# An activation tile laid out by 128-token chunks, with three additions moved from VectorE to accumulating transfers

## The chip, the cores and the metric

The kernel runs on one core of one Trainium2 chip. The metric is the device time of one execution in microseconds (us), as the median of several executions.

In the profile, PE is TensorE's matmuls, PEld its weight loads, DVE is VectorE, ACT is ScalarE, POOL is GpSimd, SP is SyncE. "L1024" is line 1024 of the kernel at hand; inserted lines shift the numbers by a few lines between kernels.

## The reference, cut to what matters

```python
# x: (1, 2048, 512), F = 1792; all in bfloat16
xn  = layernorm(x)
Bu  = einsum("bld,pd->blp", xn, B_bar)                # complex, P = 512
h_t = Lam_bar * h_{t-1} + Bu_t                        # complex scan over 2048 tokens
y   = 2 * einsum("blp,dp->bld", h, C).real + xn * Dskip
out = x + y + (silu(xn @ w1) * (xn @ w3)) @ w2
```

The kernel treats the tokens as 4 blocks of 512. Per block, the two last products, C against the states and w2 against the gates, are one long product against an "act" tile that holds 22 pieces of 128 features: the gates `silu(..)*(..)` and the real and imaginary states. Its tokens are taken as "pairs" of two 128-token chunks, 8 pairs (n = 0 to 7), two per block.

## The kernel before

A pair's product is a 2 x 2 block product done with seven products of half size in place of eight, as in Strassen's method. The left factors need sums of quarters of the act tile: S3 = A11 - A21, S2 = S3 - A22, S1 = A21 + A22 (in place) and S4 = A12 + S2 (in place on A12, so only after product 2 has read A12). Product 3 reads S4.

```python
act_blk[b] = actp.tile([P, 2 * NK, TBLK], FP16, name="act")      # 128 x 22 x 512
...
def post_c(...):                           # second part of the states, after the scans
    ...                                    # (last half of block 3: on VectorE)
        gp.dma_start(out=a, in_=p16, accum_op=ALU.add)          # "states transfer"
...
def res_list(b):                           # residual: xn*Dskip + x
    def mul(): ...                         # VectorE
    def add():
        gp.dma_start(out=xn_blk[b], in_=x_blk[b], accum_op=ALU.add)   # "residual transfer"
...
def difference(b):                         # VectorE, on the result of the residual transfer:
                                           # even chunks less odd ones, on half of the columns
    ...
        nc.vector.tensor_tensor(out=o[:, 0::2, D2]..., in0=o[:, 0::2, D2], in1=o[:, 1::2, D2], op=ALU.subtract)
...
def row_sums(n, b, p):                     # S3, S1, S2 of a pair; S3 and S2 are
    ...                                    # written over x_blk or tw
def product2():
    mms(f, v["a12"], weight(1, D1), False)
    v["s4"] = v["a12"]
    if n == 5:
        gp.dma_start(out=v["s4"], in_=v["s2"], accum_op=ALU.add)
    else:
        nc.vector.tensor_tensor(out=v["s4"], in0=v["a12"], in1=v["s2"], op=ALU.add)
```

VectorE's work of the second half of block 0 and of what follows is queued in this order (cut):

```python
ssm_tasks(0)                    # ... ends with block 0's second states transfer
...
res_tasks(0)                    # multiply, then the residual transfer of block 0
for which in (2, 0, 1): weight_sum(0, which)
res_tasks(1)
...
bg.add(*difference(0))          # needs the residual transfer of block 0
first_sums = row_sums(0, *pairs[0])
...
for i, which in ((0, 3), (1, 2), (1, 0), (1, 1), (1, 3)): weight_sum(i, which)
```

## Time and profile before

| | before |
|---|---|
| median (lowest to highest) | 201.86 us (201.84 to 201.89), 3 runs |
| profiled span | 200.1 us |
| busy: PE, DVE, ACT, POOL | 98, 91, 67, 25% of the span |
| packets of GpSimd's DMA queue | 9520 |

### The profile page before, as it was taken

To read this page: it belongs to the slowest core of one execution; us is meant where nothing else is said; L and a number is where in the kernel's file an instruction comes from. 1 tells how busy PE (TensorE), PEld (TensorE's weight loads), DVE (VectorE), ACT (ScalarE), POOL (GpSimd) and SP (SyncE) were. 2 spreads that over 40 slices of the span, in tenths; PEclk is the share of its full clock that TensorE was granted. 3 is DMA by queue.
4 is the path that set the end of the run, shared out by engine and by line. 5 is a ranking of instruction groups with operands and counts; after the bars stand their busy time and mean duration, and the time that the engine had idled before them with its cause. 6 is when DMAs were issued, how large, how long until landed. Compare 5 with 4: busy or idle time off the path is not lost.

```text
span 200.1 us, 3642 instructions
## 1 busy us (share of the span) xinstructions
PE 196.5 (98%) x1377; PEld 128.6 (64%) x1377; DVE 181.9 (91%) x255; ACT 133.9 (67%) x277; POOL 49.8 (25%) x71
## 2 busy tenths in 40 slices
PE   8999999999999999999999999999999999999994
PEld 2874444444444488854444468888566668888893
DVE  3699699999999999989999999899999999899862
ACT  3799797699999987967796684362588783111220
POOL 7170279700310132243015013100033103130000
PEclk9999999999999999999999999999999999999999
DMA  6999997990474033944876955560159901994111
GB/s 150 328 276 224 292 168 139 338 268 2 92 147 79 0 65 69 160 131 92 147 140 122 98 101 46 58 135 3 52 105 143 141 2 13 101 142 74 56 41 43
DMA packets 35651, 23.94 MB, mean 120 GB/s; under 512 B 23217, under 2 KB 33585, under 8 KB 35633
## 3 DMA queue, kind: packets, MB, share of 16 engines
q0 software_dynamic: 9520, 10.20, 34.8%
q1 hardware_dynamic: 25536, 13.21, 27.0%
q10 hardware_dynamic: 576, 0.30, 0.7%
q8 instruction: 11, 0.18, 0.4%
q14 instruction: 8, 0.06, 0.1%
HBM read 7.74 MB, written 2.10 MB: 49 GB/s over the span
## 4 chain that ended last, share of the span: by engine, by line
PE 96%; DMA 1%; DVE 1%; SPq 0%; issue 0%; DVEq 0%
PE gu_ps L555 34%; PE gu_ps L982 17%; PE y_ps L982 10%; PE gu_ps L775 7%; PE bu_ps L982 7%; PE y_ps L440 5%; PE bu_ps L440 5%; PE y_ps L797 3%; PE gu_ps L587 2%; PE gu_ps L700 2%; DMA x_blk<-in_A_x_dram 1%; PE bu_ps L797 1%; PE y_ps L700 1%; PE bu_ps L587 1%; PE y_ps L243 1%; PE bu_ps L700 0%
## 5 line engine op out<-in xcount | busy, mean ns | idle before, releaser
L555 PE MATMUL gu_ps<-xnT,w_sb 128*128 128x512 bf16 x312 | 68.2, 379 | 0.0
L555 PEld LDWEIGHTS <-w_sb 128*128 128x128 bf16 x312 | 30.4, 98 | 36.5
L982 PEld LDWEIGHTS <-act 128*128 128x128 f16 x462 | 43.5, 98 | 5.4
L565 ACT ACTIVATE u<-gu_ps 128x512 bf16<-128x512 f32 x41 | 24.8, 605 | 5.8 <-PE gu_ps L555 5.4
L564 ACT ACTIVATE g<-gu_ps 128x512 bf16<-128x512 f32 x41 | 24.7, 603 | 5.1 <-PE gu_ps L555 5.0
L488 DVE TENSOR_TENSOR_SCAN u<-rho,ends,u 128x512 bf16<-128x512 f32 x16 | 19.9, 1270 | 0.0
L507 POOL DMA_DIRECT2D act<-p x7 | 6.4, 908 | 47.1 <-DVE act L498 36.8
L440 PEld LDWEIGHTS <-bt 128*128 128x128 bf16 x96 | 9.4, 98 | 11.3
L982 PE MATMUL gu_ps<-w_sb,act 128*128 128x256 bf16 (+3 forms) x126 | 15.9, 267 | 0.0
L775 PE MATMUL gu_ps<-xnT,w_sb 128*128 128x512 bf16 x64 | 15.9, 379 | 0.0
L573 DVE TENSOR_TENSOR act<-g,u 128x1024 f16<-128x1024 bf16 x21 | 14.2, 678 | 0.0
L787 ACT ACTIVATE g<-gu_ps 128x512 bf16<-128x512 f32 x14 | 8.4, 599 | 5.4 <-PE gu_ps L775 5.0
L936 POOL DMA_DIRECT2D act<-act x4 | 7.7, 1929 | 14.6 <-DVE tw L929 13.7
L440 PE MATMUL bu_ps<-xnT,bt 128*128 128x512 bf16 x48 | 11.3, 379 | 0.0
L440 PE MATMUL y_ps<-xnT,bt 128*128 128x512 bf16 x48 | 11.3, 379 | 0.0
L1005 ACT ACTIVATE x_blk<-gu_ps 128x256 f32<-128x256 f32 (+1 forms) x9 | 3.3, 367 | 10.6 <-PE gu_ps L982 10.6
L982 PE MATMUL bu_ps<-w_sb,act 128*128 128x256 bf16 (+3 forms) x84 | 10.4, 264 | 0.0
L982 PE MATMUL gu_ps<-ct,act 128*128 128x256 f16 (+1 forms) x72 | 10.4, 267 | 0.0
L488 DVE TENSOR_TENSOR_SCAN u<-rho,act,u 128x512 bf16<-128x512 f32 x8 | 10.0, 1271 | 0.0
L494 DVE TENSOR_TENSOR p<-u,tabe 128x2048 f16<-128x2048 bf16 (+1 forms) x9 | 9.9, 1099 | 0.1
L471 DVE TENSOR_TENSOR u<-u,tabe 128x2048 bf16<-128x2048 bf16 x8 | 9.8, 1222 | 0.2
L498 DVE TENSOR_TENSOR act<-u,tabe 128x2048 f16<-128x2048 bf16 (+1 forms) x9 | 9.9, 1097 | 0.0
(189 smaller groups left out, 372.8 us busy)
## 6 DMA issues: line engine op xcount, KB each, us to landing
act<-p POOLq DMA_DIRECT2D x7, 512.0 KB, 4.7
xn<-x_blk POOLq DMA_DIRECT2D x4, 512.0 KB, 5.2
out_dram<-xn SPq DMA_DIRECT2D x15, 128.0 KB, 1.7
w_sb<-in_B_w_dram SPq DMA_DIRECT2D x1, 1792.0 KB, 8.4
w_sb<-in_B_w_dram SPq DMA_DIRECT2D x2, 768.0 KB, 6.3
act<-act POOLq DMA_DIRECT2D x4, 352.0 KB, 7.0
w_sb<-in_B_w_dram SPq DMA_DIRECT2D x4, 256.0 KB, 4.5
w_sb<-in_B_w_dram SPq DMA_DIRECT2D x2, 512.0 KB, 5.9
```

The lines of the kernel that those rows point to most:

```text
L440: nc.tensor.matmul(out=ps, lhsT=bt[:, ri, dt, pt * P:(pt + 1) * P], rhs=xnT_blk[b][:, dt, :], start=(dt == 0), stop=(dt == NDT - 1))
L471: nc.vector.tensor_tensor(out=st["g"], in0=st["g"], in1=tabe[:, psl, 0:1, :].to_broadcast(FULL), op=ALU.mult)
L488: nc.vector.tensor_tensor_scan(out=v, data0=rho[:, pt:pt + 1].to_broadcast([P, TBLK]), data1=v, initial=init, op0=ALU.mult, op1=ALU.add)
L494: nc.vector.tensor_tensor(out=st["p16"][:, :, ::-1, tsl], in0=st["g"][:, :, :, tsl], in1=tabe[:, psl, 1:3, tsl], op=ALU.mult)
L498: nc.vector.tensor_tensor(out=act_state(b, hf)[:, :, :, tsl], in0=st["g"][:, :, :, tsl], in1=tabe[:, psl, 0:1, tsl].to_broadcast([P, 2, 2, ...
L555: nc.tensor.matmul(out=ps[:, tsl], lhsT=w[:, dt, f * P:(f + 1) * P], rhs=xnT[:, dt, tsl], start=(dt == 0), stop=(dt == NDT - 1))
L564: nc.scalar.activation(out=g16[:, f % 2, :], in_=g_ps, func=ACT.Silu)
L565: nc.scalar.activation(out=u16[:, f % 2, :], in_=u_ps, func=ACT.Copy)
L573: nc.vector.tensor_tensor(out=act(b)[:, k0:k1 + 1:k1 - k0, :], in0=g16, in1=u16, op=ALU.mult)
L775: nc.tensor.matmul(out=ps, lhsT=w[:, dt, f * P:(f + 1) * P], rhs=xnT[:, dt, :], start=(dt == 0), stop=(dt == NDT - 1))
L787: nc.scalar.activation(out=g16[:, f % 2, :], in_=side(w1_sb, f), func=ACT.Silu)
L982: nc.tensor.matmul(out=out, lhsT=left[:, k, :], rhs=right[k][:, cols], start=(start and k == 0), stop=(k == NK - 1), skip_group_check=True)
```

## The change

The act tile is laid out as 4 chunks of 22 pieces of 128 tokens, so that a quarter (A11, A12, ...) becomes one run of 2816 bytes per partition instead of 11 runs of 256. This is meant to make the in-place sums cheap as accumulating transfers, so that S4 of pairs 2, 3 and 4 can leave VectorE. In pairs 2 and 3 product 2 comes ahead of product 4 to give the transfer more time. The price is that a states transfer has rows of 1024 bytes instead of 4096.

```diff
-            act_blk[b] = actp.tile([P, 2 * NK, TBLK], FP16, name="act")
+            act_blk[b] = actp.tile([P, CPB, 2 * NK, P], FP16, name="act")
...
     def act_state(b, hf):
         k = k_state(2 * hf)
-        return act(b)[:, k:k + 4, :].rearrange("p (j r) t -> p j r t", r=2)
+        return act(b)[:, :, k:k + 4, :]
...
-                a, p16 = act_state(b, hf)[:, :, :, tsl], st["p16"][:, :, :, tsl]
+                a, p16 = act_state(b, hf)[:, csl], st["p16"][:, csl]
...
-        a11, a12 = a[:, 0:NK, r1], a[:, NK:2 * NK, r1]
-        a21, a22 = a[:, 0:NK, r2], a[:, NK:2 * NK, r2]
+        a11, a12 = a[:, 2 * p, 0:NK, :], a[:, 2 * p, NK:2 * NK, :]
+        a21, a22 = a[:, 2 * p + 1, 0:NK, :], a[:, 2 * p + 1, NK:2 * NK, :]
...
-            if n == 5:
+            if n in (2, 3, 4, 5):
                 gp.dma_start(out=v["s4"], in_=v["s2"], accum_op=ALU.add)
...
-        for i in ((1, 5, 2, 6, 4, 3, 7) if b == 0 else (1, 4, 2, 6, 5, 7, 3)):
+        for i in ((1, 5, 2, 6, 4, 3, 7) if b == 0 else (1, 2, 4, 6, 5, 7, 3) if b == 1 else (1, 4, 2, 6, 5, 7, 3)):
```

The cuts are the same re-layout for the gates, the other post products of the states and the copy of the scans' last values.

More of the change, by code (lines that the diff above doesn't have):

```diff
@@ L420, in act, with act_gates, split, by_state @@
         if act_blk[b] is None:
-            act_blk[b] = actp.tile([P, 2 * NK, TBLK], FP16, name="act")
+            act_blk[b] = actp.tile([P, CPB, 2 * NK, P], FP16, name="act")
         return act_blk[b]
+    def act_gates(b, f):
+        k0, k1 = k_gate(f), k_gate(f + 1)
+        return act(b)[:, :, k0:k1 + 1:k1 - k0, :].rearrange("p c k t -> p k c t")
+    def split(v):
+        return v.rearrange("p k (c t) -> p k c t", t=P)
     def act_state(b, hf):
         k = k_state(2 * hf)
-        return act(b)[:, k:k + 4, :].rearrange("p (j r) t -> p j r t", r=2)
+        return act(b)[:, :, k:k + 4, :]
+    def by_state(v):
+        return v.rearrange("p c (j r) t -> p j r c t", r=2)
     u_blk = {}
@@ L449, in ssm_tasks, with by_chunk @@
         FULL = [P, 2, 2, TBLK]
+        def by_chunk(v):
+            return v.rearrange("p j r (c t) -> p j r c t", t=P)
         def half(hf):
@@ L485, in scan @@
                 elif b > 2:
-                    init = act_blk[b - 1][:, k_state(pt, ri), TBLK - 1:TBLK]
+                    init = act_blk[b - 1][:, CPB - 1, k_state(pt, ri), P - 1:P]
                 v = st["g"][:, j, ri, :]
@@ L489, in scan, with post_a, post_b, post_c @@
                                              initial=init, op0=ALU.mult, op1=ALU.add)
-            def post_a(tsl=slice(0, TBLK)):
+            def post_a(csl=slice(0, CPB)):
                 if "p16" not in st:
-                    st["p16"] = ssmw.tile(FULL, BF16, name="p").bitcast(FP16)
-                nc.vector.tensor_tensor(out=st["p16"][:, :, ::-1, tsl], in0=st["g"][:, :, :, tsl],
-                                        in1=tabe[:, psl, 1:3, tsl], op=ALU.mult)
-            def post_b(tsl=slice(0, TBLK)):
-                nc.vector.tensor_tensor(out=act_state(b, hf)[:, :, :, tsl], in0=st["g"][:, :, :, tsl],
-                                        in1=tabe[:, psl, 0:1, tsl].to_broadcast([P, 2, 2, tsl.stop - tsl.start]),
-                                        op=ALU.mult)
-            def post_c(tsl=slice(0, TBLK)):
-                a, p16 = act_state(b, hf)[:, :, :, tsl], st["p16"][:, :, :, tsl]
+                    st["p16"] = ssmw.tile(FULL, BF16, name="p").bitcast(FP16).rearrange(
+                        "p j r (c t) -> p (j r c t)", t=P).rearrange("p (c k t) -> p c k t", c=CPB, t=P)
+                tsl = slice(csl.start * P, csl.stop * P)
+                nc.vector.tensor_tensor(out=by_state(st["p16"][:, csl]), in0=by_chunk(st["g"][:, :, ::-1, tsl]),
+                                        in1=by_chunk(tabe[:, psl, 2:0:-1, tsl]), op=ALU.mult)
+            def post_b(csl=slice(0, CPB)):
+                tsl = slice(csl.start * P, csl.stop * P)
+                n = csl.stop - csl.start
+                nc.vector.tensor_tensor(out=by_state(act_state(b, hf)[:, csl]), in0=by_chunk(st["g"][:, :, :, tsl]),
+                                        in1=by_chunk(tabe[:, psl, 0:1, tsl]).to_broadcast([P, 2, 2, n, P]), op=ALU.mult)
+            def post_c(csl=slice(0, CPB)):
+                a, p16 = act_state(b, hf)[:, csl], st["p16"][:, csl]
                 if (b, hf) == (NBLK - 1, 1):
@@ L541, in ssm_tasks @@
         add(*post0, *scans1)
-        early, late = ([(0.6, lambda fn=fn, h=h: fn(slice(h * TH, (h + 1) * TH)), ("ssm", b)) for fn in post1]
+        early, late = ([(0.6, lambda fn=fn, h=h: fn(slice(h * CPB // 2, (h + 1) * CPB // 2)), ("ssm", b)) for fn in post1]
                        for h in range(2))
@@ L571, in gate @@
             bg.own(0.6, -0.5)
-            k0, k1 = k_gate(f - 1), k_gate(f)
-            nc.vector.tensor_tensor(out=act(b)[:, k0:k1 + 1:k1 - k0, :], in0=g16, in1=u16, op=ALU.mult)
+            nc.vector.tensor_tensor(out=act_gates(b, f - 1), in0=split(g16), in1=split(u16), op=ALU.mult)
         f0 = 0
@@ L790, in gate @@
             bg.own(0.6, -0.5)
-            k0, k1 = k_gate(f), k_gate(f + 1)
-            nc.vector.tensor_tensor(out=act(b)[:, k0:k1 + 1:k1 - k0, :], in0=tiles[0], in1=tiles[1], op=ALU.mult)
+            nc.vector.tensor_tensor(out=act_gates(b, f), in0=split(tiles[0]), in1=split(tiles[1]), op=ALU.mult)
         def product(out, left, right, start):
@@ L921, in row_sums @@
         a = act(b)
-        r1, r2 = slice(2 * p * P, (2 * p + 1) * P), slice((2 * p + 1) * P, (2 * p + 2) * P)
-        a11, a12 = a[:, 0:NK, r1], a[:, NK:2 * NK, r1]
-        a21, a22 = a[:, 0:NK, r2], a[:, NK:2 * NK, r2]
+        a11, a12 = a[:, 2 * p, 0:NK, :], a[:, 2 * p, NK:2 * NK, :]
+        a21, a22 = a[:, 2 * p + 1, 0:NK, :], a[:, 2 * p + 1, NK:2 * NK, :]
         s3, s2 = (v.bitcast(FP16).rearrange("p (k t) -> p k t", t=P) for v in homes[n % 2])
@@ L1141, in keep_ends @@
         kept.add(b)
-        nc.vector.tensor_copy(out=ends, in_=act(b).rearrange("p (h k) t -> p h k t", h=2)[:, :, NFH:NK, TBLK - 1])
+        nc.vector.tensor_copy(out=ends, in_=act(b)[:, CPB - 1].rearrange("p (h k) t -> p h k t", h=2)[:, :, NFH:NK, P - 1])
     ssm_tasks(1, between=[(0.2, lambda: keep_ends(0))])
```

## The prediction

> **What bounds the kernel now.** I read the page first, then the waits of TensorE, then the chain of waits in order of time, then the groups by shape, and last the timelines of every engine around the three pairs that change. Times on the chip: 201.86 us median, 201.84 to 201.89; the profiled span is 200.1 us, so 1.76 us lie outside it. From the page:
>
> ```profile
> PE 196.5 (98%) x1377; PEld 128.6 (64%) x1377; DVE 181.9 (91%) x255; ACT 133.9 (67%) x277; POOL 49.8 (25%) x71
> PEclk9999999999999999999999999999999999999999
> PE 96%; DMA 1%; DVE 1%; SPq 0%; issue 0%; DVEq 0%
> ```
>
> TensorE (PE) is busy 98% of the span at full clock and makes up 96% of the chain that ended last. VectorE (DVE) at 91% looks like a second bound, so the next question is whether TensorE ever waits for it. The waits of TensorE alone are one line, in the warm-up:
>
> ```profile
> PE bu_ps L196 <- PEq L1194: 0.8, 1, 0.8
> ```
>
> A busy TensorE is not yet one at its peak, so I checked the rate. Pieces of the chain, as start, length, line and count (L982 is the y products, L700 the fast Bu products of block 3 woven between them):
>
> ```profile
> 12.84 8.63 PE gu_ps L555 x40
> ...
> 117.72 1.20 PE gu_ps L982 x11
> 118.92 0.87 PE y_ps L700 x8
> 119.80 1.20 PE gu_ps L982 x11
> 121.00 0.44 PE bu_ps L700 x4
> 121.44 0.44 PE y_ps L700 x4
> 121.87 1.20 PE gu_ps L982 x11
> ...
> 126.78 2.40 PE gu_ps L982 x22
> 129.19 1.20 PE y_ps L982 x11
> ...
> 196.78 0.63 PE gu_ps L982 x11
> 197.41 0.02 issue
> 197.43 0.29 DVE xn L993
> ```
>
> 8.63/40 is 215.8 ns for a 512-column matmul, 1.20/11 is 109.1 ns for one of 256 columns. The groups by shape count 472 matmuls of 512 columns, 734 of 256 and 44 of 128 between 12.84 and 197.41 us. At (columns + 6)/2.4 ns each that is 101.87 + 80.13 + 2.46 = 184.46 us, and the chain has 197.41 - 12.84 = 184.57 us there. **All waiting of TensorE after 12.84 us adds up to 0.11 us.** Before it lies the load and the first LayerNorm, after it 2.7 us of last addition and store; the change touches neither.
>
> **What the Trainium skill says, and whether the trace agrees.** (1) "TensorE: Matmul & The Clock Gate", section Back-to-back issue gap, gives 518, 262 and 134 cycles for 512, 256 and 128 columns; the 215.8 and 109.1 ns above agree. The same section's sustained 131 ns for 512 columns is not what this trace shows, so I use the cycles. (2) "VectorE: DVE Perf Modes", section The perf-mode tier table, has a bf16 tensor_tensor of 2048 elements at 1224 ns in the 2x mode; here 1215 to 1222 ns. (3) "DMA: Bandwidth & Descriptors", section SWDGE vs HWDGE vs iDMA, says that accumulation needs a GpSimd issue; the trace has all of them on POOL. (4) The same page, section Why small descriptors are slow (HBM only), says that SBUF to SBUF transfers don't suffer from small pieces. This trace disagrees. The rates of 164 to 176 us, in 40 slices of 0.3 us:
>
> ```profile
> GB/s 27 0 0 0 0 0 0 0 0 0 0 0 0 0 0 0 0 3 81 98 99 108 108 108 105 108 106 110 187 219 167 52 9 10 17 0 218 218 218 218
> ```
>
> The long plateau near 108 is the accumulation S1 of pair 5 in 256-byte rows, the 218 at the end is the states' accumulation in 4096-byte rows.
>
> **The change, part by part.** The rows concerned, by shape:
>
> ```profile
> L1024 DVE TENSOR_TENSOR act<-act,x_blk 128x1408 f16<-128x1408 f16 x4 | 3.5, 883 | 0.0
> L1024 DVE TENSOR_TENSOR act<-act,tw 128x1408 f16<-128x1408 f16 x3 | 2.6, 883 | 1.1 <-PE bu_ps L982 0.7 <-PE gu_ps L982 0.5
> L936 POOL DMA_DIRECT2D act<-act x4 | 7.7, 1929 | 14.6 <-DVE tw L929 13.7 <-DVE u L807 0.5 <-DVE x_blk L929 0.4
> L507 POOL DMA_DIRECT2D act<-p x7 | 6.4, 908 | 47.1 <-DVE act L498 36.8 <-PE gu_ps L982 5.5 <-PE y_ps L982 4.6
> ```
>
> *Removed:* the VectorE additions S4 of pairs 2, 3 and 4, 3 x 0.883 = 2.65 us of VectorE, which falls from 181.9 to about 179.3 us. None of it is on the chain, so it is worth 0 by itself.
>
> *Layout, VectorE:* counts and element sizes stay. The innermost run becomes 128 elements of step 1. The row differences (1408 elements in runs of 128) already have such runs and take 883 to 888 ns; by the line through 678 ns at 1024 and 1216 ns at 2048 a 1408-element operation would be estimated at 680 ns + 384 x 0.525 = 880 ns. So runs of 128 cost nothing, and gates, post products and differences should keep 0.68, 1.22 and 0.88 us. Change 0.
>
> *Layout, transfers:* a row of S1 or S4 grows from 256 to 2816 bytes; a row of the states' accumulation shrinks from 4096 to 1024. With 16 engines, 108 GB/s is 37.9 ns per 256-byte row and 218 GB/s 301 ns per 4096-byte row, so as an estimate a row costs 20.4 ns + 0.0685 ns per byte. A 352 KB transfer then has 8 rows per engine of 213 ns, 1.7 us, instead of 88 of 37.9, 3.3 us. POOL's part falls from 1.93 to about 0.91 us (908 ns is the row with one piece per partition). Issue to landing: 7.0 - 1.6 - 1.0 = 4.4 us by subtraction, or 4.7 - 2.4 + 1.7 = 4.0 from the states' transfers; I take 4.0. The states' 512 KB become 32 rows per engine of 90.5 ns, 2.9 instead of 2.4 us, and POOL's part rises by 3 x 0.10 = 0.3 us: 5.5 instead of 4.7 us to landing.
>
> *Added, S4 by transfer.* Start: product 2 must have read A12. Deadline: product 3. Pair 2: product 1 (117.72, 1.20) and the woven work (0.87) put product 2 at 119.80 to 121.00. S1 of pair 3 is ahead on POOL, at 120.74, free by 121.65. S4 lands at 121.65 + 4.0 = 125.7 alone, 127.4 if it has to wait out all 1.7 us of S1's data. Product 3 starts at 127.98: 0.6 to 2.3 us to spare. Pair 3: product 2 at 131.26 to 132.46, landing 136.5, product 3 at 139.45: 2.9 us to spare. Pair 4 (its order stays, product 3 is put off into pair 5): S1 of pair 5 at 166.86, S4 at 167.8, landing 171.8 to 173.5, product 3 at 176.75: 3.2 us to spare.
>
> *Moved, product 2 ahead of 4.* Product 2 adds onto the copy that ScalarE makes of product 1. The timeline of ScalarE has these copies end at 119.39 (pair 2) and 130.85 (pair 3); product 2 would start at 119.80 and 131.26. The work woven between hides them with 0.4 us to spare each.
>
> *Deadlines that tighten:* states of block 3, first half: issued 173.37, now landing 178.1, then 178.9; TensorE reads them at 179.91. States of block 2, second half: issued 145.27, then landing 150.8; the difference that reads them starts at 151.16. Block 1: landing 105.7, read at 106.77. S1 of pair 5, needed at 175.54 and now landing at 166.86 + 7.9 = 174.8, gets room instead.
>
> Sum: at most 0.11 us to win, no stall expected: **201.86 + 0.0 = 201.9 us**.
>
> **Rivals.** *S4 lands late.* If the transfers keep 6.8 us and S1 keeps POOL for 1.93 us, S4 of pair 2 lands at 122.67 + 6.8 = 129.5, and product 3 waits 1.5 us: 203.4. For it: the spare time of pair 2 is the smallest of the three, and the one such transfer of the kernel before took 6.8 us. Against: its rows were 256 bytes, and the states' transfers with long rows took 4.7 for more bytes. *VectorE leaves its fast mode* with four-level patterns: then 14 full and 4 half post products gain about 1.07 and 0.53 us each, the 28 gates 0.53 us, together near 32 us, VectorE becomes the bound and the time nears 214. For it: no operation of the trace has that many levels, so nothing shows it; against: the differences' runs. *False waits:* states and gates now share one address range per chunk; if the program's dependency tracking took ranges as whole, a gate would wait for a 5 us transfer, which I put at 1 to 4 us in all. For it nothing but the possibility; gates at 52.22 and 54.95 ran beside a transfer begun at 51.47. *VectorE was a hidden bound* and its 2.65 us come off: 199.2, which is still within 2%; against it stands the 0.11 us.
>
> **Range and chances.** The base has a scatter of 0.05 us, and the bound allows 0.11 below it, so the low end is 201.7. Above, a missed deadline of pair 2, or of the states, would cost tenths: high end 202.5. Faster by 4 us would need matmuls removed: 0.01. Slower by 4 us needs one of the middle two rivals at its worst: 0.04. The rest, 0.95, is within 2%.
>
> **What would show it.** Right: TensorE still has no wait after the warm-up; VectorE near 179.3 us with three fewer S4 additions; S1 and S4 land in about 4 us and their POOL part is near 0.9; states' accumulation lands near 5.5 us; the 0.88, 1.22 and 0.68 us of VectorE stay. Wrong: a TensorE wait before product 3 of pair 2 (S4 late) or before product 2 of pairs 2 and 3 (copy late), post products above 1.3 us, or VectorE waiting for a transfer.

## More of the kernel before

The page's list of DMA issues names, for each kind of transfer, out<-in, the queue, the count, the size and the median time from issue to landing:

```profile
act<-p POOLq DMA_DIRECT2D x7, 512.0 KB, 4.7
xn<-x_blk POOLq DMA_DIRECT2D x4, 512.0 KB, 5.2
```

The first is the states transfer, the second the residual transfer.

## The result

| | before | after |
|---|---|---|
| median (lowest to highest) | 201.88 us (201.84 to 202.13), 4 runs | 202.85 us (202.50 to 203.16), 4 runs |
| ratio, 95% interval | | 1.0045 (1.0026 to 1.0064) |
| profiled span | 200.1 us | 201.1 us |
| VectorE busy | 181.9 us | 179.9 us |
| packets of GpSimd's DMA queue | 9520 | 6240 |

A ratio here is the mean time of one kernel's runs over that of the other's runs of the same rounds, so it is not quite the ratio of the medians quoted.

The change costs about 1 us, where 0.0 was predicted. It is within the 2% that counts as the same, and yet outside the predicted range of 201.7 to 202.5 us, and the interval of the ratio lies above 1. So there is something real to find.

**Is there a new wait?** The page of the changed kernel, its busy times and its chain of waits by engine:

```profile
PE 196.0 (98%) x1365; PEld 128.6 (64%) x1377; DVE 179.9 (89%) x252; ACT 134.2 (67%) x277; POOL 49.3 (25%) x74
...
PE 59%; DVE 17%; issue 8%; POOL 7%; DMA 6%; ACT 1%; POOLq 0%
```

TensorE is still busy 98% of the span, but the chain that ended last is no longer TensorE's alone: 17% of it runs through VectorE, 7% through GpSimd and 6% through transfers. Something between them holds TensorE up. (The page counts 12 matmuls fewer than before and as many weight loads, 1377: those are records missing from the trace, and no work was removed.) The waits of TensorE in the changed kernel (engine, instruction, what released it; total, times, longest):

```profile
PE bu_ps L196 <- PEq L1207: 0.8, 1, 0.8
PE bu_ps L995 <- DVE act L1037: 0.5, 1, 0.5
PE gu_ps L571 <- DMA xnT<-xn: 0.4, 1, 0.4
```

The first is the warm-up, which the kernel before has too. The other two are new. Their place in TensorE's timeline of the changed kernel (start, length, engine, line, operation, tiles; in brackets the idle time before it and its releaser):

```profile
74.18 1.36 PE L995 MATMUL y_ps<-tw,act 128*128 128x256 f16 x11
76.06 0.94 PE L995 MATMUL bu_ps<-w_sb,act 128*128 128x256 bf16 x7 [0.51 <-DVE act L1037]
...
87.40 5.79 PE L571 MATMUL gu_ps<-xnT,w_sb 128*128 128x512 bf16 x25 [0.36 <-DMA xnT<-xn]
```

The same two places in the kernel before:

```profile
74.46 1.36 PE L982 MATMUL y_ps<-tw,act 128*128 128x256 f16 x11
75.66 0.93 PE L982 MATMUL bu_ps<-w_sb,act 128*128 128x256 bf16 x7
...
86.47 6.86 PE L555 MATMUL gu_ps<-xnT,w_sb 128*128 128x512 bf16 x31
```

A matmul's end is drawn later than the start of the next, so starts are what to subtract. Before, product 3 of pair 0 starts 1.20 us after the product ahead of it, and after the change 76.06 - 74.18 = 1.88 us: 0.68 us lost. The gate matmuls of block 2 start at 87.40, where the group ahead of them (at 85.67, of 1.20) would have let them start at 86.87: 0.53 us lost. Together that is 1.21 us. **Both places lie in pairs 0 and 1, far from pairs 2, 3 and 4, whose S4 was changed.** The first wait is for VectorE's S4 of pair 0, which the change leaves on VectorE.

To be independent of the start-up, I count the time from the start of the first 512-column matmul to the start of the last group of four matmuls, and call it the steady part: 12.67 to 197.01 = 184.34 us before, 12.40 to 197.93 = 185.53 us after. The difference of 1.19 us is the two waits.

**Why is VectorE late?** Its timeline before, around the half difference of block 0's residual (L876) and S4 of pair 0 (L1024):

```profile
57.69 1.29 DVE L405 TENSOR_TENSOR ct<-ct,tw 128x1024 f16<-128x1024 f16 x2
58.89 0.42 DVE L876 TENSOR_TENSOR xn<-xn 128x512 f16<-128x512 bf16 x1
...
74.08 0.88 DVE L1024 TENSOR_TENSOR act<-act,x_blk 128x1408 f16<-128x1408 f16 x1
```

And after:

```profile
57.44 1.29 DVE L405 TENSOR_TENSOR ct<-ct,tw 128x1024 f16<-128x1024 f16 x2
59.91 0.43 DVE L890 TENSOR_TENSOR xn<-xn 128x512 f16<-128x512 bf16 x1 [1.19 <-DMA xn<-x_blk]
...
75.11 0.89 DVE L1037 TENSOR_TENSOR act<-act,x_blk 128x1408 f16<-128x1408 f16 x1
```

VectorE now waits 1.19 us for the residual transfer, and S4 of pair 0 comes 1.03 us later although TensorE was 0.28 us earlier: it ends at 76.00, and product 3, due at 74.18 + 1.20 = 75.38, starts at 76.06. Before, it ended at 74.96 with 0.70 us to spare. There was nothing in between to soak up the delay. In the kernel before, the view by stretches has, from the difference to S4 (length, then busy time and instructions of PE, PEld, DVE, ACT and POOL):

```profile
58.85:74.08 15.23, 15.23 (x92) 8.88 (x91) 15.09 (x23) 14.88 (x38) 1.64 (x4) 1.00 0.23 43
```

VectorE is busy 15.09 of 15.23 us there, so an instruction late at 58.9 is as late at 74.1.

**Why is the residual late?** Nothing about its own layout changed. GpSimd's timeline before, with the issues of block 0's second states transfer and of the residual transfer:

```profile
51.47 0.86 POOL L507 DMA_DIRECT2D act<-p  x1 [12.25 <-DVE act L498]
52.60 0.85 POOL L865 DMA_DIRECT2D xn<-x_blk  x1 [0.26 <-DVE xn L861]
```

After:

```profile
51.22 1.28 POOL L523 DMA_DIRECT2D act<-p  x1 [11.79 <-DVE act L515]
52.35 1.06 POOL L879 DMA_DIRECT2D xn<-x_blk  x1
```

The residual is issued 1.13 us behind the states in both kernels, on the same queue. The landings, which the views give to 0.1 us, are read from the trace's own times here: before, the states take 4.6 us (to 56.03) and the residual 6.2 us (to 58.77); after, 5.5 us (to 56.70) and 7.5 us (to 59.89). The difference can't start before the residual lands. Before, it started at 58.89, so this transfer had some 0.1 us to spare and no wait showed.

The rates of 50 to 60 us, in 40 slices of 0.25 us, first before, then after, show what the residual waits for:

```profile
GB/s 0 0 0 0 0 0 0 0 0 0 0 197 147 180 262 229 147 147 262 229 66 229 262 197 115 213 262 262 180 82 262 262 0 66 0 0 0 16 246 246
```

```profile
GB/s 0 0 0 0 0 0 0 0 0 0 0 0 78 172 160 180 172 168 184 164 160 164 168 184 217 221 229 262 147 147 229 262 164 180 164 17 66 246 246 229
```

Before, both transfers run at some 200 GB/s, and only a last piece comes after 58.0. After, there is a plateau of 160 to 184 GB/s from 53.0 to 56.0, which is the states with rows of 1024 bytes, and the residual's faster data come behind it. From the states' issue to the residual's landing it is 58.77 - 51.47 = 7.30 us before and 59.89 - 51.22 = 8.67 us after. Slices of 25 and 60 ns put the first data at 52.90 before and 53.07 after, and the last at 58.38 and 58.98. So the 1.37 us more have three parts. From the issue to the first data it is 0.42 us more, as much as GpSimd's part for the states grew (0.86 to 1.28). The stream of data is 0.43 us longer (5.48 to 5.91). From the last data to the landing it is about 0.5 us more (0.4 to 0.9), which I can't divide further.

That one transfer starts behind the other in the queue agrees with the Trainium skill, "DMA: Bandwidth & Descriptors", section Two DMAs through the same engine are not ordered: within one queue of a DMA engine, descriptors start in order.

**What the change was made for works.** Groups of the changed kernel, by shape: the transfers S1 (L949) and the states (L523) on GpSimd, and one of the two kinds of S4 left on VectorE.

```profile
L523 POOL DMA_DIRECT2D act<-p x7 | 9.3, 1328 | 29.4 <-DVE act L515 29.2 <-issue 0.2
L949 POOL DMA_DIRECT2D act<-act x4 | 4.1, 1021 | 13.8 <-DVE tw L942 13.3 <-DVE x_blk L942 0.5
...
L1037 DVE TENSOR_TENSOR act<-act,x_blk 128x1408 f16<-128x1408 f16 x2 | 1.8, 888 | 0.5 <-PE gu_ps L995 0.5
```

GpSimd's part of an S1 fell from 1929 to 1021 ns in the mean. The transfers of S4 land ahead of the products that read them: pair 2 at 122.23 + 4.6 = 126.8 for product 3 at 128.92, pair 3 at 133.69 + 4.0 = 137.7 for 140.38, pair 4 at 168.53 + 6.4 = 174.9 for 177.84. No TensorE wait appears there, neither for S4 nor for ScalarE's copy of product 1.

### The profile page after: what moved, and what is told of

The parts are those of the page before. It is cut to its first block, busy times and chain, and to the rows that moved or that the text cites. A ratio compares the mean times of both kernels' runs of the same rounds, so it can differ in the third digit from the quotient of the medians.

```text
span 201.1 us, 3636 instructions
## 1 busy us (share of the span) xinstructions
PE 196.0 (98%) x1365; PEld 128.6 (64%) x1377; DVE 179.9 (89%) x252; ACT 134.2 (67%) x277; POOL 49.3 (25%) x74
## 3 DMA queue, kind: packets, MB, share of 16 engines
q0 software_dynamic: 6240, 11.28, 33.4%
## 4 chain that ended last, share of the span: by engine, by line
PE 59%; DVE 17%; issue 8%; POOL 7%; DMA 6%; ACT 1%; POOLq 0%
PE gu_ps L995 13%; PE gu_ps L571 12%; PE y_ps L995 7%; PE gu_ps L790 7%; PE bu_ps L995 5%; DMA xn<-x_blk 4%; PE y_ps L811 3%; DMA xnT<-xn 3%; PE bu_ps L196 2%; DVE act L588 2%; PE y_ps L450 2%; PE bu_ps L450 2%; PE gu_ps L715 2%; DVE tw L919 1%; DVE tw L376 1%
## 5 line engine op out<-in xcount | busy, mean ns | idle before, releaser
L571 PEld LDWEIGHTS <-w_sb 128*128 128x128 bf16 x312 | 30.4, 98 | 37.0 <-DMA xnT<-xn 0.6
L523 POOL DMA_DIRECT2D act<-p x7 | 9.3, 1328 | 29.4 <-DVE act L515 29.2
L790 PEld LDWEIGHTS <-w_sb 128*128 128x128 bf16 x64 | 6.3, 98 | 4.8
```

The source lines that it names most:

```text
L571: nc.tensor.matmul(out=ps[:, tsl], lhsT=w[:, dt, f * P:(f + 1) * P], rhs=xnT[:, dt, tsl], start=(dt == 0), stop=(dt == NDT - 1))
L790: nc.tensor.matmul(out=ps, lhsT=w[:, dt, f * P:(f + 1) * P], rhs=xnT[:, dt, :], start=(dt == 0), stop=(dt == NDT - 1))
```

## The experiments

The theory, A: the layout of block 0 alone makes the loss, because its second states transfer holds up the residual transfer behind it, on which VectorE and then product 3 of pair 0 wait. The first rival, B: the S4 transfers and the new order of products cost the time, by what they do to queues and engines. Later rivals were C, that the second TensorE wait, for the transposes of block 2, has a cause of its own, and D, that the two transfers cost the same together in whichever order they are issued.

Runs e1 to e4 were made in one job on one chip, e5 to e7 in another, e8 to e10 in a third, each beside runs of the kernel before on that chip. All gave correct results.

| run | median (lowest to highest), us | before, same chip | ratio (95%) | steady part, us |
|---|---|---|---|---|
| e1_layout_only | 203.10 (202.85 to 204.15) | 201.94 | 1.0070 (1.0037 to 1.0104) | 185.52 |
| e2_s4_only | 206.19 (205.84 to 206.51) | 201.94 | 1.0206 (1.0185 to 1.0226) | 188.37 |
| e3_block0_old | 201.83 (201.63 to 202.04) | 201.94 | 0.9990 (0.9973 to 1.0008) | 184.44 |
| e4_block0_only | 203.01 (202.41 to 203.29) | 201.94 | 1.0045 (1.0022 to 1.0068) | 185.08 |
| e5_difference_later | 203.18 (202.94 to 203.66) | 201.92 | 1.0055 (1.0039 to 1.0072) | 185.46 |
| e6_transfers_swapped | 202.48 (202.13 to 204.78) | 201.92 | 1.0049 (1.0007 to 1.0090) | 184.98 |
| e7_both_mended | 202.32 (201.52 to 202.53) | 201.92 | 1.0013 (0.9996 to 1.0029) | 184.30 |
| e8_wait_filled | 201.84 (201.49 to 201.99) | 201.95 | 0.9987 (0.9960 to 1.0013) | 184.30 |
| e9_shorter_rows | 205.56 (205.27 to 207.07) | 201.95 | 1.0185 (1.0145 to 1.0224) | 187.80 |
| e10_changed_again | 203.02 (202.80 to 203.18) | 201.95 | 1.0043 (1.0013 to 1.0073) | 185.61 |

The steady part is read from the one profiled execution of each run. The start-up ahead of it ended between 12.18 and 13.20 us, without regard to the kernel, which would explain why medians scatter more than the steady part does.

### e1_layout_only: the layout without the S4 transfers and the new order

```diff
-            if n in (2, 3, 4, 5):
+            if n == 5:
...
-        for i in (... if b == 0 else (1, 2, 4, 6, 5, 7, 3) if b == 1 else (1, 4, 2, 6, 5, 7, 3)):
+        for i in (... if b == 0 else (1, 4, 2, 6, 5, 7, 3)):
```

> The chunked Act layout alone: S4 of pairs 2, 3 and 4 is back on VectorE and product 2 back behind product 4. Theory A (the loss comes from the layout: the states' transfer of block 0 in 1024-byte rows slows the residual transfer beside it, VectorE waits 1.2 us for that one, and TensorE some 1.0 us later): 202.6 to 203.1 us, VectorE waiting about 1.2 us for the residual transfer near 59 us, TensorE waiting about 0.5 us each for S4 of pair 0 and for the transposes of block 2. Theory B (the loss comes from S4 by transfer or from the order of the products): 201.9 us, no such waits.

Measured: 203.10 us, ratio 1.0070. VectorE waits 1.1 us for the residual transfer, TensorE 0.4 us for S4 of pair 0 and 0.4 us for the transposes of block 2, and the steady part is 185.52 us, as in the changed kernel. What follows: the layout alone makes the loss, and the S4 transfers and the order are worth nothing either way when they stand on it. B falls.

### e2_s4_only: the S4 transfers and the order, in the old layout

The act tile of every block is allocated as before and only viewed by chunks:

```diff
+            if b < 9:
+                act_blk[b] = actp.tile([P, 2 * NK, TBLK], FP16, name="act").rearrange("p k (c t) -> p c k t", t=P)
+            else:
                 act_blk[b] = actp.tile([P, CPB, 2 * NK, P], FP16, name="act")
```

The buffer p of the states is treated likewise, and post_c issues the transfer with rows of 4096 bytes as before.

> The old Act layout in all blocks, but S4 of pairs 2, 3 and 4 by transfer and product 2 ahead of product 4. Theory A: nothing is lost before 100 us; S4 of pair 2 has 256-byte rows, so by the first rival of the prediction it lands at about 129.5 us, product 3 of pair 2 waits about 1.5 us and the time is about 203.4 us. If instead POOL or the transfer is quicker than that, 201.9 us. Theory B (the S4 transfers or the order lose the 1.0 us whatever the layout): about 202.9 us with the TensorE waits near 75 and 87 us that the changed kernel has.

Measured: 206.19 us, ratio 1.0206. It was more than either theory had put down. S4 of pair 2, issued at 121.81, lands 7.6 us later at 129.4, and TensorE waits 0.93 us for it at 129.42, the only wait I had foreseen. In block 3, S1 of pair 5 (issued at 168.43), S4 of pair 4 (169.51) and a states transfer (170.93) now lie behind one another on the queue, the first two with rows of 256 bytes. The states land 12.5 us after their issue, at 183.4, and VectorE waits for them:

```profile
DVE x_blk L951 <- DMA act<-p: 4.6, 1, 4.6
```

TensorE loses another 1.23 us to S4 of pair 4, 0.27 to the states and 0.83 to ScalarE there. No wait is seen at 75 or 87 us. So the long rows are what makes the S4 transfers harmless: without them the same change costs over 4 us. (The S1 transfers keep their short rows here as well, so this run doesn't tell S1's share from that of S4.)

### e3_block0_old: the changed kernel, with block 0 in the old layout

The edit is that of e2 with the condition `b == 0`.

> The changed kernel, only block 0 keeps the old Act layout (states transfer in 4096-byte rows); blocks 1 to 3 are chunked and S4 of pairs 2, 3 and 4 goes by transfer. Theory A: 201.9 us, the residual transfer of block 0 lands in 5.2 to 5.9 us as before, no wait of VectorE for it, no wait of TensorE after the warm-up. A rival (the chunked layout costs in every block, or the S4 transfers cost): 202.5 us or more.

Measured: 201.83 us, ratio 0.9990. TensorE has no wait after the warm-up, the states land in 4.6 us and the residual in 6.3 us, and the steady part is 184.44 us. The whole loss is undone by the layout of one block out of four.

### e4_block0_only: the kernel before, with block 0 alone in the new layout

The edit is that of e2 with the condition `b > 0`, and that of e1.

> The kernel before, only block 0 has the chunked Act layout. Theory A: 202.6 to 203.1 us with the same three waits as the changed kernel. The rival that the layout costs in every block: about a quarter of the loss, 202.1 us. Theory B: 201.9 us.

Measured: 203.01 us, ratio 1.0045, the same ratio as the whole change. VectorE waits 1.0 us for the residual transfer; TensorE 0.3 us for S4 of pair 0. The third wait is too short for the list of TensorE's waits, but by the starts it is there: the gate matmuls of block 2 start at 86.88, and the group ahead of them (at 85.39, of 1.20) would have let them start at 86.59. The steady part, 185.08 us, has 0.74 of the 1.19 us; the profile fell on the fastest of the four runs. With e3 this shows both ways that block 0's layout is the cause.

### e5_difference_later: the difference moved behind the row sums

The difference of block 0 is not needed until later, so I moved it behind the row sums of pair 0, on the idea that those don't need the residual transfer.

```diff
-    bg.add(*difference(0))
     first_sums = row_sums(0, *pairs[0])
...
     bg.add(*first_sums[2])
+    bg.add(*difference(0))
```

> The changed kernel with one VectorE instruction (the residual's half difference of block 0, which waits 1.2 us for the residual transfer) queued behind the three row sums of pair 0 that follow it; all transfers stay as they are. Theory A (the loss is VectorE standing still for that transfer, and both TensorE waits follow from it): the residual transfer still lands in about 7.5 us, VectorE no longer waits for it, TensorE waits neither for S4 of pair 0 nor for the transposes of block 2: 201.9 us. Rival C (the second TensorE wait, for the transposes of block 2, comes from slower transfers of its own): the first wait goes, the second of 0.4 us stays: about 202.4 us.

Measured: 203.18 us, ratio 1.0055. This was a miss. The wait moves to the next instruction:

```profile
DVE x_blk L942 <- DMA xn<-x_blk: 1.1, 1, 1.1
```

The row sum S3 of pair 0 is written over x_blk, which the residual transfer still reads. Two instructions in a row wait for the same transfer, once for what it writes and once for what it reads, and the waits' list shows only the first. Both TensorE waits stay (0.44 and 0.36 us).

### e6_transfers_swapped: the residual issued ahead of the states

```diff
-            add(*pre0, *scans0, *post0, *pre1, *scans1, *post1)
+            add(*pre0, *scans0, *post0, *pre1, *scans1, *post1[:2])
+            put_off.append((0.0, post1[2], ("ssm", b)))
...
     res_tasks(0)
+    bg.add(*put_off.pop())
```

> The changed kernel with the second states transfer of block 0 issued behind the residual transfer of block 0 and not before it. Theory A (the residual transfer is late because it shares the engines with the states transfer of 1024-byte rows ahead of it): the residual transfer lands in about 4.6 to 5.5 us, the wait of 1.2 us goes, the states have until the row sum at about 61 us: 201.9 us. Rival D (the row length itself is not the matter, any neighbour costs the same): the states transfer now lands late and VectorE waits for it instead, about 202.5 to 202.9 us.

Measured: 202.48 us, with one run at 204.78, ratio 1.0049 with a wide interval (1.0007 to 1.0090). The residual now lands in 4.7 us, but the states, issued at 53.21, land 7.8 us later at 61.0, and VectorE waits for them a little further on:

```profile
DVE act L950 <- DMA act<-p: 0.9, 1, 0.9
```

TensorE's waits shrink (0.24 us for the transposes, 0.4 us of weight loads for S4) and the steady part falls to 184.98 us, about halfway. So the order decides who waits, and whichever comes second lands at about 60 to 61 us: what grew is the sum of the two transfers, as D has it. D's other half, that the row length is not the matter, falls with e3: from the first issue to the last landing the same two transfers take 7.4 us there, with the old rows, against 8.7 in the changed kernel and 8.3 here.

### e7_both_mended: e3 and e5 together

> The changed kernel with block 0 in the old layout and the residual's difference queued later: more room on both sides. TensorE has no wait left to remove but some 0.1 us, so no theory expects it below the kernel before: 201.8 to 201.9 us, ratio 0.999 to 1.001. Below 201.5 us would mean that the kernel before had a wait that its profile doesn't show.

Measured over 5 rounds: 202.32 us (201.52 to 202.53), ratio 1.0013 (0.9996 to 1.0029), some 0.4 us above what I had expected. The steady part is 184.30 us, and TensorE's only waits are in the start-up, one of them 0.9 us for the load of w_sb, which the profile of the kernel before doesn't have. I read the excess as scatter of the start-up, which was 0.5 us longer (13.19 against 12.67 us) in this profile; one profile per kernel can't prove it. In any case there is no gain to be had from moving the difference.

### e8_wait_filled: the whole change, with other work in VectorE's wait

One weight sum, a VectorE operation of 1.08 us that needs none of these transfers, is moved ahead of the difference. All four blocks stay in the new layout.

```diff
+    weight_sum(0, 3)
     bg.add(*difference(0))
...
-    for i, which in ((0, 3), (1, 2), (1, 0), (1, 1), (1, 3)):
+    for i, which in ((1, 2), (1, 0), (1, 1), (1, 3)):
```

> The changed kernel with one independent weight sum of 1.08 us (the fourth of the gate weights, needed only by product 4 of pair 0) moved ahead of the first instruction that waits for the residual transfer; all transfers as they are. In e5 the wait did not go, because the next instruction, the first row sum of pair 0, writes its result over the x tile that the same transfer reads. Theory A: VectorE now waits 0.0 to 0.3 us there and not 1.2 us, S4 of pair 0 is ready about 1 us earlier, TensorE waits neither for it nor for the transposes of block 2: 201.9 us. Rival C (the wait for the transposes has a cause of its own, the slower states transfers or another one): the wait for S4 goes, that of about 0.4 us for the transposes stays: 202.3 us.

Measured over 5 rounds: 201.84 us, ratio 0.9987. The residual still takes 7.6 us to land; only VectorE no longer stands idle for it:

```profile
DVE xn L890 <- DMA xn<-x_blk: 0.2, 1, 0.2
```

S4 of pair 0 starts at 73.88, TensorE has no wait after the warm-up, and the steady part is 184.30 us. The late transfer costs nothing by itself: it costs what VectorE idles. The wait for the transposes of block 2 is gone as well, so it was a consequence of VectorE's delay, and C falls.

### e9_shorter_rows: more of the suspected cost

Block 0's second states transfer is split into four, one per chunk, with rows of 256 bytes.

```diff
+                elif (b, hf) == (0, 1):
+                    for c in range(CPB):
+                        gp.dma_start(out=a[:, c], in_=p16[:, c], accum_op=ALU.add)
```

For this half alone, p is kept in the old order.

> A larger dose: the changed kernel with the second states transfer of block 0 cut into four transfers with rows of 256 bytes (same bytes). By the row costs of the prediction its data take 4.9 us and not 2.9, and POOL's part for four of them, an estimated 4.8 us and not 1.3, holds the issue of the residual transfer back. Theory A: the residual transfer lands 1.6 us or more later than in the changed kernel, VectorE waits about 2.8 us or more, and the time grows by the same amount, to 204.4 us or a little more. If the loss has nothing to do with when that transfer lands: 202.9 us as the changed kernel.

Measured: 205.56 us, ratio 1.0185, which is 2.5 us above e10 on the same chip and about 1 us above what I had expected. GpSimd needs 5.21 us for the four, the residual is issued at 54.43 and lands 8.5 us later at 62.9, and VectorE waits:

```profile
DVE xn L897 <- DMA xn<-x_blk: 4.0, 1, 4.0
```

TensorE waits 1.98 us for S4 of pair 0. Counted from the states' issue, the residual landed 2.8 us later than in e10, and TensorE's first wait grew by about 1.5 us; a further wait of 0.86 us for ScalarE near it is new, and I did not trace where it comes from. The sign and the place are as A has them, the size only roughly. The run changes GpSimd's part and the rows together and can't tell them apart.

### e10_changed_again: the changed kernel beside e8 and e9

> The changed kernel as it is, again, beside the two on the same chip: 202.5 to 203.2 us, with the waits of its first profile (VectorE about 1.2 us for the residual transfer, TensorE about 0.5 us for S4 of pair 0 and 0.4 us for the transposes of block 2).

Measured: 203.02 us, ratio 1.0043, with VectorE's wait of 1.2 us and TensorE's of 0.5 and 0.5 us. The loss repeats on another chip.

## Why the prediction was right or wrong

**The bound: right.** TensorE sets the end in both kernels, but for the two waits, and removing VectorE work was worth 0: e1, with the three S4 on VectorE, and e10, with them as transfers, have steady parts of 185.52 and 185.61 us.

**Removed work: right for its worth, a little off in size.** VectorE's busy time fell by 2.0 us and not by 2.65. Operations overlap a little in the timeline (one begins at 57.69 with 1.29 us, the next at 58.89), so a sum of means overstates busy time; the rest of the 0.6 us I did not resolve.

**Layout on VectorE: right.** The full post products take 1217 ns, the gates 679 ns and S4 880 to 888 ns. The rival of a lost fast mode is out, and so are the false waits between states and gates: no gate waits for a transfer.

**Layout of the transfers: right for the states and GpSimd, too short for S1 and some of S4.** The states were put at 5.5 us and their median was 5.6; GpSimd's part for them at about 1.2 us and it was 1.33 in the mean (1.28 to 1.47); S1's and S4's part at 0.91 and it was 0.85 to 0.88 for most of them (1.02 in the mean of S1). The landing of S4, put at 4.0 us, took 3.8 to 6.4, with the longest where others were in flight; S1, put at about 4 as well, took 3.8 to 5.8.

**S4 by transfer: right.** Pair 2 had 2.1 us to spare (0.6 to 2.3 were predicted), pair 3 had 2.7 (2.9) and pair 4 had 2.9 (3.2). S4 of pair 2 was issued ahead of S1 of pair 3 (122.23 and 122.77), not behind it as the prediction assumed, which did no harm.

**"Deadlines that tighten", and with it "no stall expected": the step that failed.** It went through the states of blocks 1, 2 and 3 and asked of each whether its own landing comes before its own reader. It left out block 0, and it never asked what lies behind a states transfer in the same queue. Block 0's second states transfer has the residual transfer 1.13 us behind it, and that one had about 0.1 us to spare. The states arrived later by about what was predicted. That was enough, with what it did to the neighbour, for the residual to land 1.37 us later after the states' issue, for VectorE to idle 1.19 us, and for TensorE to lose 0.68 and 0.53 us. Of the signs that the prediction named for being wrong, the last one came, VectorE waiting for a transfer.

**A size was also short.** With the prediction's own terms (0.3 us more of GpSimd, 0.5 us more data) the residual would have come 0.8 us later. Less 0.1 us to spare at VectorE and 0.70 us at TensorE, that estimate leaves no stall at all. So a reader who had listed this pair would have found a step with no room left, though not the 1.2 us. The data term was about right (0.43 us), GpSimd's part grew by 0.42, and the 0.5 us between last data and landing were in no term.

**What is shown and what is argued.** e3, e4 and e8 show that block 0's layout, through VectorE's wait, makes both TensorE waits. That the second comes about because the later u<-p transfer (issued at 79.92 before and 80.96 after) overlaps the transposes is my reading of the timelines. What speaks for it is the last of the four transposes. In the five profiles where u<-p is issued 2.6 us behind the first transpose (the kernel before, e2, e3, e7, e8), the four take 8.7 to 9.1 us from first issue to last landing; in the seven where it is 3.8 us (the changed kernel, e1, e4, e5, e6, e9, e10), they take 9.9 to 10.3. In the kernel before the last one lands at 86.42, and TensorE, ready at 86.47, starts there at once: this deadline had no room either, and no list of waits shows it. No run moves u<-p alone, so that link stays argued. The prediction's base scatter of 0.05 us was also too narrow: over 29 further runs of the kernel before on three chips, its times lay between 201.50 and 203.22 us.

**The range.** It had 201.7 to 202.5, and 0.6 us above the centre for "a missed deadline"; the delay passed through two TensorE waits and not one. The chance of 0.95 for a time within 2% held, with 1.0045. The version that keeps the layout everywhere and fills the wait (e8, 201.84 us) is level with the kernel before, which is where the prediction put the change.

## What to carry to other kernels

When a change makes one transfer longer, look not only at who reads it but at what is issued next on the same queue, and at how much that neighbour has to spare; a wait list of the kernel before showed nothing here while 0.1 us was left. In this case an engine at 91% busy, with next to no idle time between a delayed instruction and the one that the bounding engine needs, passed the delay on in full. Such a wait can be filled with work that was queued for later, which here gave back all of the loss (e8).

## What the Trainium skill lacked or had wrong

- "DMA: Bandwidth & Descriptors", section Why small descriptors are slow (HBM only), says that SBUF to SBUF transfers don't suffer. For accumulating ones that does not hold here: they ran at about 108 GB/s with rows of 256 bytes, 160 to 184 with 1024 and 218 with 4096. No run has a plain copy within SBUF to compare.
- The same page, section Anatomy of one DMA — SWDGE (gpsimd) path, fits 2.0 us + bytes / 436e3, an estimate of 3.2 us for 512 KB; the states transfer with the longest rows took 4.6 us. That one accumulates, of which the section doesn't speak. It calls descriptor generation small; GpSimd's part was 0.86, 1.28 and 1.93 us for 1, 4 and 11 rows per partition.
- The same page says that descriptors within a queue start in order, and no page has a figure for what one transfer's rows cost the transfer behind it: here the residual landed 1.37 us later after the states' issue.
- "TensorE: Matmul & The Clock Gate", section Back-to-back issue gap, has a sustained 131 ns for 512 columns beside its cycles; here it is 215.8 ns, which agrees with the cycles alone.
